# Nine more idle products of the identity in each early pause of TensorE

## The chip, the cores and the metric

The kernel runs on one core of one Trainium2 chip. The metric is the device time of one execution in microseconds (us). The time before the change is 676.36 us, the median of 3 runs that lie between 675.13 and 676.87 us.

## What is computed

Local attention with a summary of every block, then a two-layer feed-forward network, in float32:

```python
# q, k, v: (4, 8, 768, 64); w_in: (512, 2048); w_out: (2048, 512)
k_sum = k.reshape(B, H, nb, block, D).max(axis=3)
v_sum = v.reshape(B, H, nb, block, D).mean(axis=3)
scores_l = scale * np.matmul(q, k.transpose(0, 1, 3, 2))     # kept where |i - j| < 16
scores_s = scale * np.einsum('bhsd,bhnd->bhsn', q, k_sum) + np.log(block)
a = softmax(concatenate([scores_l_masked, scores_s]))
x = matmul(a, concatenate([v, v_sum]))                       # reshaped to (3072, 512)
h = x @ w_in
g = h * (1.0 / (1.0 + np.exp(-h)))
return g @ w_out
```

## The kernel before

**Tiles.** The 3072 tokens are cut into 24 stages of 128 tokens for the attention and into 12 chunks of 256 tokens for the network. A stage computes scores of a pair of heads (line 602, later 593 or 595 and 596), the softmax (VectorE line 609, ScalarE line 612, the scaling at 623, 625 or 627), turns the weights round (lines 636 and 638 on TensorE, or a transposing DMA at line 654) and multiplies with v (lines 668 or 683). Two stages fill one chunk x, which is kept as a high and a low part (xh at lines 696 and 701, xl at lines 697 and 702). The network walks over 16 slices f of the hidden layer: twelve matmuls of the first layer into a bank h (line 757), tanh and product on ScalarE and VectorE (767, 768, 769), six matmuls of the second layer (762). The weights come in 64-bit form and are decoded on ScalarE and VectorE (716 to 723, 256 to 263).

**Order.** Nothing runs in the order of the source. Every piece is given to a planner as an operation with its engines, its cost and what it reads and writes. `sweep` walks through planned time and gives each engine its sequence; `issue` then writes the instructions in the order of planned start, and each engine runs its own sequence in that order. Semaphores hold an instruction until its data are there. DMAs are issued by SyncE (SP), also in one sequence.

**Idle products.** Where the plan leaves TensorE without work it puts in matmuls whose result nobody reads: the identity, read as 16-bit numbers, times itself, 128x256. They exist so that TensorE is not idle. In the early part, before the first operation of the network, each pause gets as many as fit, counted at 110 ns each, and they write bank 0 (line 333). Afterwards only pauses ahead of the network's first layer get them, and they write the bank h that this layer is about to write (line 766), so they wait until the last reader of that bank is done. In the program there are 131 of them in 11 places: 15, 17, 1, 19, 2, 8, 1 and 18 at line 333, then 19, 20 and 11 at line 766. Pause 1 is the place with the first 15, pause 10 the place with the 20. In the sequence of TensorE an idle product stands like any other instruction: whatever is behind it starts after it, even if its data have come.

The number of products is the last entry of a planned operation:

```python
for _ in range(fills):
    (self.ops[i][6] or self.fill)()
self.ops[i][1](e)
```

Of the kernel before, what the change touches and what calls it, by code (L numbers as in the profile page):

```python
# [87 lines left out]
class Plan:  # L88
# [10 lines left out]
    BUSY = 3072.0  # L99
    FILL = (110.0, 256.0)  # L100
    GUARD = 150.0
    FIRST = 3000.0
    ROUNDS = 6
    SPARE = 100
# [41 lines left out]
    def sweep(self, prio, on, back):  # L146

        n = len(self.ops)
        before, after = [o[2] for o in self.ops], self.users
        if back:  # L150
            before, after = after, before
        left = [len(d) for d in before]
        end, chosen = [0.0] * n, [None] * n
        free = {} if back else {"dma": 1680.0}
        shared = 0.0
        ready, seen, fills, filled, early, order = {}, {}, 0, self.FIRST, True, []

        def arrive(i):
            ready[i] = {e: max([end[d] + (self.lag(e, chosen[d], d) if back else self.lag(chosen[d], e, i)) for d in before[i]], default=0.0)
                        for e in ((on[i],) if on else self.ops[i][0])}  # L160

        for i in range(n):
            if not left[i]:
                arrive(i)
        while ready:
            best = None
            for i, ts in ready.items():
                for e, s in ts.items():
                    f = free.get(e, 0.0)
                    t = max(s, f, shared) if e in self.ops[i][5] else max(s, f)  # L170
                    wait = self.SPARE if e == "dve" and len(ts) > 1 and t < self.RUSH else 0.0
                    key = (max(t + wait, f + self.PATIENCE), prio[i], t + self.ops[i][0][e], i)
                    if best is None or key < best[0]:
                        best = (key, i, e, t)
            _, i, e, t = best
            del ready[i]
            cost, cols = self.ops[i][0][e], self.ops[i][4]
            fills = 0
            if e == "pe" and not back:
                early = early and cols < self.BUSY  # L180
                if early or self.ops[i][6]:
                    while True:
                        rate = 1.0 if seen.get(int(filled / self.TICK) - 1, 0.0) >= self.BUSY else 0.5
                        if filled + self.FILL[0] / rate + self.GUARD > t:
                            break
                        filled = self.stream(seen, filled, *self.FILL)
                        fills += 1
                stop = self.stream(seen, t, cost, cols)
                filled = stop
            else:  # L190
                stop = t + cost * (1.0 if e in ("pe", "dma") else self.MARGIN)
            end[i], chosen[i] = stop, e
            free[e] = stop
            if e in self.ops[i][5]:
                shared = stop
            order.append((t, stop, i, e, fills))
            for u in after[i]:
                left[u] -= 1
                if not left[u]:
                    arrive(u)  # L200
        return order
# [727 lines left out]
```

## Time and profile before

| | us |
|---|---|
| median of the runs (lowest, highest) | 676.36 (675.13, 676.87) |
| the profiled execution, as timed | 675.26 |
| its span, first to last instruction | 673.5 |
| TensorE (PE) busy | 657.9 |
| VectorE (DVE) busy | 490.1 |
| ScalarE (ACT) busy | 428.0 |
| GpSimd (POOL) busy | 198.3 |

The busy time of TensorE holds the idle products too. The mean granted clock of TensorE over the span is 0.989 of full speed; 1.00 is 2.4 GHz and 0.50 is 1.2 GHz. Times in the rows below are counted from the start of the span.

### The profile page before, as it was taken

The numbers are of one execution on the slowest core, as the hardware profiler recorded it, in microseconds if no ns is written. First come the engines' busy times: TensorE is split into PE (matmuls) and PEld (weight loads), VectorE is DVE, ScalarE is ACT, GpSimd is POOL, SyncE is SP. The second block draws the span as 40 slices with busy tenths as digits, with TensorE's granted clock in tenths as the row PEclk, the third lists the DMA queues.
The fourth block names the chain that finished last, engine by engine and source line by source line (L and its number), as shares of the span: only waits on it lengthen the run. The fifth ranks groups of instructions, "written<-read, shape, count | busy, mean of one in ns | idle before, by whom it ended". The sixth has DMA issues, their size and how long they took to land.

```text
span 673.5 us, 14263 instructions
## 1 busy us (share of the span) xinstructions
PE 657.9 (98%) x4995; PEld 572.4 (85%) x4995; DVE 490.1 (73%) x1538; ACT 428.0 (64%) x1122; POOL 198.3 (29%) x241
## 2 busy tenths in 40 slices
PE   7988999999999999999999999999999999999997
PEld 4666899887988898888988898888898888899996
DVE  6886978688899646887888755897899986433332
ACT  4977999788867754666755554765776853322322
POOL 3241255333343111332535141223335333000000
PEclk9987999999999999999999999999999999999999
DMA  8689793976654842573664752573744642100000
GB/s 299 223 237 277 272 313 109 238 202 179 165 155 130 230 132 83 150 173 78 182 155 121 194 170 78 125 188 92 178 125 139 158 88 40 44 1 1 32 0 33
DMA packets 101354, 97.42 MB, mean 145 GB/s; under 512 B 76950, under 2 KB 80022, under 8 KB 101282
## 3 DMA queue, kind: packets, MB, share of 16 engines
q1 hardware_dynamic: 101282, 96.51, 52.4%
q8 instruction: 39, 0.64, 0.4%
q14 instruction: 33, 0.27, 0.1%
HBM read 70.34 MB, written 6.29 MB: 114 GB/s over the span
## 4 chain that ended last, share of the span: by engine, by line
PE 92%; DVE 3%; ACT 2%; DMA 2%; issue 0%; SPq 0%; POOL 0%; ACTq 0%; POOLq 0%
PE bank L757 41%; PE bank L762 39%; PE bank L683 4%; PE bank L595 2%; PE bank L596 2%; DMA qk<-in_qkT_dram 1%; PE bank L593 1%; DMA raw<-in_kD_dram 1%; PE bank L526 1%; PE bank L766 1%; DVE e L609 1%; DVE p L651 1%; PE bank L602 1%; ACT e L612 0%; PE bank L333 0%
## 5 line engine op out<-in xcount | busy, mean ns | idle before, releaser
L757 PE MATMUL bank<-xh,wt 128*128 128x256 f32 x1536 | 309.8, 285 | 0.0
L757 PEld LDWEIGHTS bank<-xh,wt 128*128 128x128 f32 x1536 | 252.5, 191 | 8.2 <-issue 0.4
L762 PE MATMUL bank<-wt,gh 128*128 128x512 f32 x768 | 247.3, 403 | 0.0
L757 PE MATMUL bank<-xl,wt 128*128 128x256 f32 x768 | 217.8, 284 | 0.3 <-DVE xl L697 0.3
L263 POOL TENSOR_TENSOR gl<-t,gh 128x256 fp32r<-128x256 f32 x123 | 108.7, 884 | 320.3 <-ACT gh L769 245.9
L767 ACT ACTIVATE t<-bank 128x256 f32<-128x256 f32 x192 | 73.3, 382 | 125.2 <-PE bank L757 123.5
L757 PEld LDWEIGHTS bank<-xl,wt 128*128 128x128 f32 x768 | 147.1, 192 | 6.8 <-DVE xl L697 0.5
L768 DVE SCALAR_TENSOR_TENSOR t<-t,bank 128x256 f32<-128x256 f32 x192 | 80.0, 417 | 99.4 <-ACT t L767 98.0
L762 PE MATMUL bank<-wt,gl 128*128 128x512 f32 x384 | 150.2, 391 | 1.0 <-POOL gl L263 1.0
L762 PEld LDWEIGHTS bank<-wt,gh 128*128 128x128 f32 x768 | 129.8, 190 | 17.5 <-issue 0.6
L769 ACT CAST gh<-t 128x256 fp32r<-128x256 f32 x192 | 77.8, 406 | 64.5 <-DVE t L768 62.9
L651 DVE SCALAR_TENSOR_TENSOR p<-e,sum,p 128x128 f16<-128x128 f32 x352 | 115.4, 389 | 1.3 <-ACT p L623 0.8
L612 ACT ACTIVATE e<-e,mx 128x182 f32<-128x182 f32 x192 | 84.4, 442 | 12.6 <-DVE mx L609 12.2
L762 PEld LDWEIGHTS bank<-wt,gl 128*128 128x128 f32 x384 | 72.1, 188 | 18.1 <-POOL gl L263 1.7
L263 DVE TENSOR_TENSOR gl<-t,gh 128x256 fp32r<-128x256 f32 x69 | 30.7, 444 | 34.4 <-ACT gh L769 20.0
L609 DVE CUSTOM_DVE_ANT_0 e<-bank,masks,qsc 128x182 f32<-128x182 f32 x144 | 52.2, 400 | 2.8 <-PE bank L596 2.4
L625 POOL TENSOR_SCALAR p<-e,sum 128x182 f16<-128x182 f32 x46 | 23.2, 509 | 46.5 <-DVE sum L618 18.2
L612 ACT ACTIVATION_READ_ACCUMULATOR e<-e,mx 128x1 f32 x192 | 36.7, 191 | 0.0
L263 POOL TENSOR_TENSOR vv<-raw,vv 128x1024 f16<-128x1024 f32 x15 | 32.5, 2170 | 7.6 <-ACT vv L256 7.2
L683 PEld LDWEIGHTS <-vv 128*64 128x64 f16 x880 | 25.7, 111 | 5.6 <-issue 4.6
L595 PE MATMUL bank<-qk 128*128 128x182 f16 x144 | 28.7, 246 | 0.0
L498 DVE SCALAR_TENSOR_TENSOR qk<-raw,qsc,qk 64x1264 f16<-64x1264 f32 x18 | 28.0, 1555 | 0.7
(127 smaller groups left out, 696.8 us busy)
## 6 DMA issues: line engine op xcount, KB each, us to landing
wt<-in_w_dram SPq DMA_DIRECT2D x32, 512.0 KB
raw<-in_kD_dram SPq DMA_DIRECT2D x18, 632.0 KB
raw<-in_v_dram SPq DMA_DIRECT2D x20, 512.0 KB
raw<-in_qD_dram SPq DMA_DIRECT2D x18, 512.0 KB
out_dram<-raw SPq DMA_DIRECT2D x24, 256.0 KB
raw<-in_kF_dram SPq DMA_DIRECT2D x12, 384.0 KB
raw<-in_qF_dram SPq DMA_DIRECT2D x9, 512.0 KB
raw<-in_vR_dram SPq DMA_DIRECT2D x12, 384.0 KB
```

The costliest lines, as they stand in the source:

```text
L263: eng[e].tensor_tensor(out=out, in0=in0, in1=in1, op=ALU.subtract)
L498: plan.op({"dve": 1450}, lambda e: nc.vector.scalar_tensor_tensor(out=kst[64:, :, :NLOC], in0=kr[64:], scalar=qs[64:, 1:2], in1=kst[64:, : ...
L595: nc.tensor.matmul(out=sc[:, i, :NKEY], lhsT=qh[:, h, :], rhs=kst[:, h, :], start=True, stop=False)
L609: plan.op({"dve": 258 if b == 0 else 323}, lambda e, i=i: nc.vector.tensor_tensor_reduce(out=et[:, i, :], in0=sc[:, i, :NKEY], in1=mask, s ...
L612: plan.op({"act": 431}, lambda e, i=i, h=h: nc.scalar.activation(out=et[:, i, :], in_=et[:, i, :], func=AF.Exp, scale=-1.0, bias=mx[:, i:i ...
L651: nc.vector.scalar_tensor_tensor(out=pt[:, i, to:to + z - a], in0=et[:, i, a:z], scalar=su[:, i:i + 1], in1=pt[:, i, a:z], op0=ALU.mult, o ...
L683: nc.tensor.matmul(out=av[j * D:(j + 1) * D, i * P:(i + 1) * P], lhsT=vt[:, vi, h * D:(h + 1) * D], rhs=tt[:, j * 3 + blk, :], start=(n == ...
L757: nc.tensor.matmul(out=h, lhsT=wt[f, 0][:, part, ct * P:(ct + 1) * P], rhs=x[:, ct, :], start=(ct == 0 and q == 0), stop=(ct == NCT - 1 an ...
L762: nc.tensor.matmul(out=bank[ob[u]], lhsT=g[:, u * P:u * P + P], rhs=wt[f, 1][:, part, :], start=(opens and q == 0), stop=(closes and q == 2))
L767: plan.op({"act": 264}, lambda e: nc.scalar.activation(out=t, in_=h, func=AF.Tanh, scale=0.5), r=[("bank", k)], w=[("t", j)], prio=i - TUN ...
L768: plan.op({"dve": 335}, lambda e: nc.vector.scalar_tensor_tensor(out=t, in0=t, scalar=1.0, in1=h, op0=ALU.add, op1=ALU.mult), r=[("bank", ...
L769: plan.op({"act": 307}, lambda e: nc.scalar.copy(out=gh, in_=t), r=[("t", j)], w=[("gh", n)], prio=i - TUNE["post"])
```

## The change

Whenever a pause got at least one product and the operation behind it is planned to start before 75,000 ns, nine more products (1000 divided by 110, rounded down) are added to the count. They are added after the plan has worked out its times, so that the planned times do not know of them.

```diff
@@ class Plan
     GUARD = 150.0
+    OVER, BUSIER = 1000.0, 75000.0
     FIRST = 3000.0
@@ def sweep
                         filled = self.stream(seen, filled, *self.FILL)
                         fills += 1
+                    if fills and t < self.BUSIER:
+                        fills += int(self.OVER / self.FILL[0])
                 stop = self.stream(seen, t, cost, cols)
```

Pauses 1 to 10 get nine more each, pause 11 none: 131 products become 221. Apart from them the sequence of every engine is what it was, and the lines of the changed kernel are three higher (333 is 336, 602 is 605, 757 is 760).

TensorE at pause 3, in the middle of the early attention, between a small transpose for the scale of v and the turning round of softmax weights (`ident` is the identity, `e` the softmax weights, bank_199 is bank 0). Before:

```order
L431 MATMUL bank_205<-ident,am 1x128
L333 LDWEIGHTS ident
L333 MATMUL bank_199<-ident 128x256
L636 MATMUL bank_202<-ident,e_174 128x128 x2
L638 MATMUL bank_202<-ident,e_174 54x128 x2
```

The same place in the changed kernel:

```order
L434 MATMUL bank_205<-ident,am 1x128
L336 LDWEIGHTS ident
L336 MATMUL bank_199<-ident 128x256
...
L639 MATMUL bank_202<-ident,e_174 128x128 x2
L641 MATMUL bank_202<-ident,e_174 54x128 x2
```

The line of dots stands for nine more pairs of a weight load and a product: one product has become ten, and nothing else stands there.

TensorE at pause 10, between the scores of a stage (`qk` holds q and k) and the first layer for the third slice (`wt` the weights, `xh` the chunk). Before, with 19 more pairs in place of the dots:

```order
L602 MATMUL bank_203<-qk_150 128x182
L602 MATMUL bank_204<-qk_150 128x182
L766 LDWEIGHTS ident
L766 MATMUL bank_199<-ident 128x256
...
L757 MATMUL bank_199<-xh_184,wt 128x256
```

In the changed kernel, with 28 more pairs in place of the dots:

```order
L605 MATMUL bank_203<-qk_150 128x182
L605 MATMUL bank_204<-qk_150 128x182
L769 LDWEIGHTS ident
L769 MATMUL bank_199<-ident 128x256
...
L760 MATMUL bank_199<-xh_184,wt 128x256
```

Twenty products have become 29, all of them on the bank that the first layer behind them writes.

## Rows read from the trace of the kernel before

**Rows 1.** The page: busy time by engine, and engines' shares of the last chain
```profile
PE 657.9 (98%) x4995; PEld 572.4 (85%) x4995; DVE 490.1 (73%) x1538; ACT 428.0 (64%) x1122; POOL 198.3 (29%) x241
...
PE 92%; DVE 3%; ACT 2%; DMA 2%; issue 0%; SPq 0%; POOL 0%; ACTq 0%; POOLq 0%
```

**Rows 2.** Waits of TensorE from 64 us on: us, times, longest
```profile
PE bank L762 <- POOL gl L263: 1.0, 1, 1.0
```

**Rows 3.** Stretches: us, busy by engine (instructions), granted clock, DMA share, GB/s
```profile
24.00:28.00 4.00, 4.00 (x36) 3.30 (x34) 3.85 (x21) 3.83 (x13) 0.00 (x0) 1.00 0.49 163
...
44.00:48.00 4.00, 1.86 (x6) 1.49 (x6) 3.49 (x14) 3.44 (x8) 0.86 (x1) 0.59 0.94 292
48.00:52.00 4.00, 4.00 (x48) 3.78 (x49) 1.67 (x3) 1.42 (x3) 0.00 (x0) 0.55 1.09 289
...
56.00:60.00 4.00, 3.71 (x18) 2.58 (x18) 4.00 (x17) 4.00 (x13) 1.13 (x2) 0.50 1.29 298
```

**Rows 4.** TensorE in order of time, 0 to 20 us: start, duration, instruction, [idle before]
```profile
1.36 3.38 PE L333 MATMUL bank<-ident 128*128 128x256 bf16 x15 [1.36 <-POOL ident masks.py:199]
7.58 1.58 PE L602 MATMUL bank<-qk 64*128 64x182 f32 x8 [2.84 <-ACT qk L256]
9.10 2.75 PE L333 MATMUL bank<-ident 128*128 128x256 bf16 x17
11.78 1.04 PE L526 MATMUL bank<-wt,blocks 128*24 128x512 f32 x2
```

**Rows 5.** Half microseconds of pause 2, idle products alone
```profile
9.50:10.00 0.50, 0.50 (x4) 0.38 (x3) 1.00 1.07 390
...
11.00:11.50 0.50, 0.50 (x7) 0.44 (x6) 1.00 1.08 376
```

**Rows 6.** TensorE in order of time, 20 to 75 us
```profile
23.50 2.24 PE L333 MATMUL bank<-ident 128*128 128x256 bf16 x19
25.59 0.44 PE L636 MATMUL bank<-ident,e 128*128 128x128 f32 x2
...
27.15 1.04 PE L333 MATMUL bank<-ident 128*128 128x256 bf16 x8
28.34 0.89 PE L602 MATMUL bank<-qk 64*128 64x182 f32 x8
...
46.14 1.55 PE L593 MATMUL bank<-qk 64*128 64x182 f32 x4 [2.96 <-DMA qk<-in_qkT_dram]
...
56.29 4.42 PE L766 MATMUL bank<-ident 128*128 128x256 bf16 x20 [3.19 <-DVE t L768]
60.37 0.56 PE L757 MATMUL bank<-xh,wt 128*128 128x256 f32 x1
...
62.62 0.88 PE L593 MATMUL bank<-qk 64*128 64x182 f32 x4
```

**Rows 7.** ScalarE and then VectorE in order of time, early instructions
```profile
11.01 0.62 ACT L530 ACTIVATE raw<-wt 128x512 f32<-128x512 f32 x1
...
25.10 0.43 ACT L623 ACTIVATE e<-e,sum 128x182 f32<-128x182 f32 x1
...
27.86 0.42 DVE L260 COPY wt<-bank 128x256 f32<-128x256 f32 x1
...
31.76 0.35 DVE L609 CUSTOM_DVE_ANT_0 e<-bank,masks 128x182 f32<-128x182 f32 x1 [0.55 <-PE bank L602]
```

**Rows 8.** Chain that ended last, 0 to 70 us: start, duration, what
```profile
42.28 3.72 DMA qk<-in_qkT_dram
...
47.69 2.87 PE bank L757 x12
50.58 0.02 ACT t L767
...
55.91 0.34 DVE t L768
...
65.09 1.43 PE bank L757 x12
```

## The prediction

> **What bounds the kernel now.** I read the page first: TensorE is busy for 98% of the span and carries 92% of the chain that ended last [rows 1]. Then the waits of TensorE after the early part: from 64 us to the end there is a single one that is long enough to be listed, 1.0 us [rows 2]. So whatever time TensorE stands at when it gets to 64 us, it keeps to the end: nothing behind that point can give back a delay of several microseconds, and nothing is cheaper there. The question is only how late, or how early, TensorE leaves the first 64 us.
>
> In those 64 us TensorE has three real pauses: 2.84 us before the first scores [rows 4], 2.96 us at 46.14 (a DMA of q and k) and 3.19 us at 56.29 (VectorE's step on the first bank h) [rows 6]. The granted clock is low there too: 0.59 and 0.55 in the stretches from 44 to 52 us, and 0.50 from 56 to 60 us [rows 3]. Everywhere else between 9 and 43 us TensorE runs without a listed wait, because the idle products fill the pauses. What has to be found out is whether they fill them with room to spare or to the brim.
>
> **Price of a product.** Nineteen of them stand between 23.50 and the next instruction at 25.59 [rows 6]: 2.09/19 = 0.110 us at full clock. At the low clock fifteen take 3.38 us [rows 4]: 0.225 us. Nine more are therefore 0.99 us at full and 2.0 us at half clock.
>
> **Pause 1: nothing.** The 15 products end at 1.36 + 3.38 = 4.74, and the scores start at 7.58, after 2.84 us of waiting for ScalarE [rows 4]. Even 2.0 us more end before that. Without that cover they would cost 2.0.
>
> **Pause 2: +0.99.** The 17 products go from 9.10 to 11.78, where the matmul of line 526 follows without a wait [rows 4]. Its block of v is in place earlier: ScalarE's line 530 reads the same block from 11.01 on [rows 7]. So this pause is already overfilled, and nine more come on top. The lower bound is a clock gain. Products run at four in half a microsecond at 9.5 us and at seven at 11.0 us [rows 5], so the clock is granted in between (the clock column holds no record before that change and prints 1.00). If pause 1 being busier brings this forward to before 7.58, the scores take 0.89 [rows 6] in place of 1.58 us [rows 4], and 26 products take 2.86 in place of 2.68: 0.5 us earlier. I take +0.99, since the row shows the clock rising only within TensorE's first long unbroken run and pause 1 still ends in a wait.
>
> **Pauses 3 to 7: +4.64.** Behind pause 4, line 636 starts at 25.59; the softmax weights it needs come from ScalarE's line 623, which ends at 25.10 + 0.43 = 25.53. Behind pause 6, the scores start at 28.34; VectorE's line 260, which clears their bank, ends at 27.86 + 0.42 = 28.28 [rows 6, 7]. The pauses are filled to 0.06 us. Five times nine products are 4.95 us, less the little room in pause 6: its eight products end at 27.15 + 8 x 0.110 = 28.03, which leaves 0.31. Can the others take this up? VectorE and ScalarE are busy for 3.85 and 3.83 of 4.00 us at 24 to 28 us [rows 3], and VectorE's line 609 at 31.76 sits idle for 0.55 us until the scores ahead of it are done [rows 7]. So they fall behind with TensorE. The cost is between +1.0 (see the second rival) and +4.95.
>
> **Pauses 8 and 9: nothing.** They lie between 33 and 41 us and cost TensorE 1.98 us, but behind them stands the wait of 2.96 us at 46.14, which ends when a DMA issued at 42.28 lands [rows 6, 8]. That DMA stands in SyncE's sequence behind the transposes of VectorE's softmax weights, so it moves with VectorE (by the terms above), not with these two pauses. The wait shrinks from 2.96 to about 1.0 us. Without that cover: +1.98.
>
> **Pause 10: +0.99.** Its 20 products do not fill the wait of 3.19 us at all: they write the bank that VectorE's line 768 still reads, so the first one starts after it, at 56.29, and the first layer follows at 60.37 [rows 6]. Everything here is in TensorE's own way. These 20 run at half clock. If the clock rises at the same time as before, the nine more push network matmuls out of the slow stretch as far as they fall into it themselves, so the price is that at full clock, 0.99. The upper bound is 2.0.
>
> **Clock at 46 us: -2.11.** After the wait of 2.96 us the stretches from 44 to 52 us ran at 0.59 and 0.55 [rows 3]. With a wait of about 1.0 us I expect the clock to hold. Then line 593 takes 0.88 (as at 62.62) in place of 1.55, and twelve matmuls of line 757 take 1.43 (as at 65.09) in place of 2.87 [rows 6, 8]: 0.67 + 1.44 = 2.11 us. This is on the path: ScalarE's line 767 starts at 50.58, as these twelve end at 47.69 + 2.87 = 50.56, and the chain goes on through ScalarE and VectorE to line 768, which releases pause 10 [rows 8]. The bounds are 0 and -2.11.
>
> [...]
>
> **Sum.** 0.99 + 4.64 + 0.99 - 2.11 = +4.51 us. On the profiled execution's 675.26 us that is 679.8; that execution is 1.1 us below the median of the runs, on which it would be 680.9. I say **680.0 us**, slower.
>
> **Rivals.** *First, the clock gives nothing back.* Where the clock falls depends on where TensorE's busy and idle stretches lie, and a wait of 1.0 us may still cost it. Then the sum is +6.62: 681.9. For it: 0.59 came after a wait of the same kind. Against it: that one was three times as long.
>
> *Second, the pauses swallow it.* The recorded chain has pieces of DMA, ScalarE and VectorE ahead of the waits at 46.14 and 56.29 [rows 8]. If those engines have room and do not fall behind, the DMA lands at 46.0 as before. But TensorE's own work has then grown by 0.99 + 4.64 + 1.98 = 7.6 us against a wait of 2.96, so it still comes to line 593 about 4.6 us late; with the clock held (line 593 and the twelve, -2.11) it is 2.5 us late at the next wait, and that one, 3.19 us, takes it all. Pause 10's 0.99 remains: 676.3, no change that can be measured. The point from which it decides is whether VectorE's line 609 is late by less than the wait it feeds. For it: TensorE is not on the chain just before 46 us. Against it: line 609's idle 0.55 us and the starts within 0.06 us.
>
> *Third, not slower at all.* As the second, and the clock also holds through the shortened wait before pause 10. Then 29 products take 3.19 us in place of the 4.08 from 56.29 to 60.37, and the twelve behind them run at full clock from the first (between 60.37 and 62.62 they took up to 2.25, less 1.43 is 0.8): -0.9 - 0.8 = -1.7 us, 673.6. It needs all of it at once: VectorE not late and the clock held in both places.
>
> *That the change does nothing* is excluded: 90 products more stand in TensorE's sequence.
>
> **Chances and range.** My forecast, between +2.5 (the clock also granted earlier in pause 2, some room on VectorE) and +5.6 us (pause 10 at half clock), 0.58; first rival 0.20; second 0.14; third 0.08. The forecast's own range is 677.8 to 681.9 with the higher median taken in. Over 0.3%, which is 2.0 us and about what runs spread over 1.7 us can tell from no change, are slower: the first rival and nearly all of the forecast, 0.76; within: the second and bits of its neighbours, 0.17; faster: the part of the third that reaches beyond its 1.7, 0.07. For 8 in 10 I go from 676.5, which takes in most of the second rival, to 682.8, the first rival with most of the median's 1.1.
>
> **What would show it.** Pause 2 right: line 529 (526 before) starts about 12.8 us, or 11.3 if the clock came early. Pauses 3 to 7 right: VectorE's line 612 (609 before) waits longer for the scores, and VectorE's and ScalarE's busy shares between 24 and 36 us fall. Pauses 8 and 9 right: the wait before line 596 (593 before) shrinks to 1 us and the DMA ahead of it is issued about 5.5 us later. Clock right: over 0.9 in the 5 us behind that wait. Pause 10 right: its products still start only behind VectorE's line 771. The forecast is wrong if TensorE's second-layer matmuls reach their unbroken run at the same time as before, or if waits appear behind 64 us.

## The result

The changed kernel takes 678.98 us (median of 16 runs, 676.97 to 681.66), the kernel before 674.98 us on the same chip (16 runs, 672.43 to 676.87): ratio 1.0064, interval [1.0049, 1.0080], that is +4.3 us [3.3, 5.4]. It is slower, by about the 4.5 us of the sum.

Executions of one and the same kernel can lie 4 to 8 us apart here, and one trace is one of them. The recorded execution of the changed kernel is the fastest of its 16 (676.97 us, span 675.2); the one of before (675.26 us, span 673.5) is a usual one by its time. So the two traces differ by 1.7 us only. Below, the traces tell what each step does, the medians what it costs. Two executions of the run with ten products in pause 10, at 1622 and 3602 us, are left out of its ratio.

The page of the changed kernel, the rows that answer to [rows 1]:

```profile
PE 663.2 (98%) x5085; PEld 577.4 (86%) x5085; DVE 494.7 (73%) x1538; ACT 426.4 (63%) x1122; POOL 197.6 (29%) x241
...
PE 87%; DVE 5%; DMA 4%; ACT 1%; SPq 1%; issue 1%; POOL 0%; ACTq 0%; DVEq 0%
```

TensorE is 5.3 us busier (663.2 against 657.9), though 90 products at 0.110 us are 9.9 us: most of the rest is work that ran at the full clock instead of the half one, as the rows below show piece by piece. Its share of the chain falls from 92 to 87%. Ahead of the wait for q and k the chain passes through VectorE and the DMA in both kernels, past pauses 8 and 9; what is new is that it comes there from TensorE's scores behind pause 7 (ends at 35.80), where before it came through ScalarE's line 612 (from 30.04).

Waits of TensorE in the first 64 us of the changed kernel (us, times, longest):

```profile
PE bank L769 <- DVE t L771: 2.1, 1, 2.1
PE bank L605 <- ACT qk L259: 1.8, 1, 1.8
PE bank L596 <- DMA qk<-in_qkT_dram: 1.4, 1, 1.4
...
PE bank L686 <- DMA wt<-p: 0.9, 1, 0.9
```

All three long waits of before are shorter (2.8, 3.0 and 3.2 us there [rows 4, 6]), and one is new, before line 686. From 64 us on no wait is listed at all.

For the steps, four more rows of TensorE in the kernel before, in order of time (start, duration, instruction):

```profile
30.84 0.89 PE L602 MATMUL bank<-qk 64*128 64x182 f32 x8
...
42.90 0.28 PE L757 MATMUL bank<-xh,wt 128*128 128x256 f32 x1
...
50.48 1.81 PE L683 MATMUL bank<-wt,vv 128*64 128x128 f16 x40
...
63.43 0.73 PE L762 MATMUL bank<-wt,gh 128*128 128x512 f32 x2
```

and TensorE in the changed kernel, the same places:

```profile
1.36 4.30 PE L336 MATMUL bank<-ident 128*128 128x256 bf16 x24 [1.36 <-POOL ident masks.py:199]
7.42 0.89 PE L605 MATMUL bank<-qk 64*128 64x182 f32 x8 [1.76 <-ACT qk L259]
8.24 3.01 PE L336 MATMUL bank<-ident 128*128 128x256 bf16 x26
11.18 1.04 PE L529 MATMUL bank<-wt,blocks 128*24 128x512 f32 x2
...
34.86 0.89 PE L605 MATMUL bank<-qk 64*128 64x182 f32 x8
...
48.34 0.28 PE L760 MATMUL bank<-xh,wt 128*128 128x256 f32 x1
49.99 0.85 PE L596 MATMUL bank<-qk 64*128 64x182 f32 x4 [1.38 <-DMA qk<-in_qkT_dram]
...
52.38 1.03 PE L686 MATMUL bank<-wt,vv 128*64 128x128 f16 x30
54.36 0.47 PE L686 MATMUL bank<-wt,vv 128*64 128x128 f16 x10 [0.95 <-DMA wt<-p]
...
58.15 4.99 PE L769 MATMUL bank<-ident 128*128 128x256 bf16 x29 [2.15 <-DVE t L771]
62.90 0.36 PE L760 MATMUL bank<-xh,wt 128*128 128x256 f32 x1
...
64.50 0.88 PE L596 MATMUL bank<-qk 64*128 64x182 f32 x4
```

Start against start (after less before), this is a ledger of the delay between the two traces:

| place in TensorE's sequence | before | after | late by | step |
|---|---|---|---|---|
| line 526 / 529, behind pause 2 | 11.78 | 11.18 | -0.60 | -0.60 |
| scores behind pause 7 | 30.84 | 34.86 | +4.02 | +4.62 |
| last matmul before the wait for q and k | 42.90 | 48.34 | +5.44 | +1.42 (pauses 8, 9) |
| scores behind that wait | 46.14 | 49.99 | +3.85 | -1.59 (wait) |
| weights times v, line 683 / 686 | 50.48 | 52.38 | +1.90 | -1.95 (clock) |
| products of pause 10 | 56.29 | 58.15 | +1.86 | -0.04 |
| first layer behind them | 60.37 | 62.90 | +2.53 | +0.67 |
| next scores, line 593 / 596 | 62.62 | 64.50 | +1.88 | -0.65 |

From the last line to the end of the span both kernels need the same: 673.5 - 62.62 = 610.9 and 675.2 - 64.50 = 610.7 us. So the difference of the traces arises ahead of 64 us, and nothing behind gives more than 0.2 us of it back.

The ledger compares one execution with one. The traces of the experiments below say how far such a step is a draw. Line 526 / 529 / 530 (first row) starts between 11.54 and 12.87 us in the nine traces whose pauses 1 and 2 are those of before (middle one 12.46; the trace of before, 11.78, is an early one), and at 11.01, 11.15, 11.18 and 13.23 in the four that have nine more in both. From the scores behind the wait for q and k to the weights times v (fourth to fifth row) it is 4.34 us before and 2.39 in the changed kernel.

Stretches of the changed kernel, with the columns of [rows 3]:

```profile
24.00:28.00 4.00, 4.00 (x37) 3.47 (x35) 3.11 (x17) 2.24 (x9) 0.00 (x0) 1.00 0.75 214
...
48.00:52.00 4.00, 2.62 (x20) 2.24 (x19) 3.55 (x14) 3.36 (x8) 0.85 (x1) 1.00 1.07 359
52.00:56.00 4.00, 2.76 (x52) 2.15 (x52) 2.52 (x5) 3.27 (x7) 0.00 (x0) 1.00 1.17 286
56.00:60.00 4.00, 1.85 (x15) 1.51 (x14) 4.00 (x20) 4.00 (x14) 2.00 (x3) 0.89 1.12 287
60.00:64.00 4.00, 4.00 (x26) 3.23 (x25) 4.00 (x14) 3.72 (x8) 0.52 (x2) 0.69 1.12 326
```

VectorE and ScalarE fell from 3.85 and 3.83 busy us to 3.11 and 2.24 between 24 and 28 us: they wait for scores that now come later, behind the idle products. The granted clock is 1.00 from 48 to 56 us, where it was 0.55 from 48 to 52 before. The two stretches in which pause 10 lies show 0.89 and 0.69.

### The profile page after: what moved, and what is told of

It reads as the page before. It is cut to its first block, busy times and chain, and to the rows that moved or that the text cites. A ratio compares the mean times of both kernels' runs of the same rounds, so it can differ in the third digit from the quotient of the medians.

```text
span 675.2 us, 14443 instructions
## 1 busy us (share of the span) xinstructions
PE 663.2 (98%) x5085; PEld 577.4 (86%) x5085; DVE 494.7 (73%) x1538; ACT 426.4 (63%) x1122; POOL 197.6 (29%) x241
## 4 chain that ended last, share of the span: by engine, by line
PE 87%; DVE 5%; DMA 4%; ACT 1%; SPq 1%; issue 1%; POOL 0%; ACTq 0%; DVEq 0%
PE bank L760 37%; PE bank L765 36%; PE bank L686 3%; PE bank L598 2%; PE bank L336 2%; DVE p L654 2%; PE bank L599 2%; DMA raw<-in_qF_dram 1%; DMA qk<-in_qkT_dram 1%; PE bank L596 1%; PE bank L769 1%; DMA raw<-in_v_dram 1%; PE bank L529 1%; DMA raw<-in_qD_dram 1%; DVE e L612 1%
## 5 line engine op out<-in xcount | busy, mean ns | idle before, releaser
L266 POOL TENSOR_TENSOR gl<-t,gh 128x256 fp32r<-128x256 f32 x123 | 106.7, 867 | 321.7 <-ACT gh L772 247.3
L266 DVE TENSOR_TENSOR gl<-t,gh 128x256 fp32r<-128x256 f32 x69 | 32.8, 475 | 32.9 <-ACT gh L772 19.1
L266 POOL TENSOR_TENSOR vv<-raw,vv 128x1024 f16<-128x1024 f32 x15 | 33.9, 2262 | 7.7 <-ACT vv L259 7.3
```

The costliest lines, as they stand in the source:

```text
L266: eng[e].tensor_tensor(out=out, in0=in0, in1=in1, op=ALU.subtract)
```

## The experiments

Every kernel is the kernel before with a table of extra products by pause, added where the instructions are issued; the rest of every engine's sequence stays as it is. Its lines are four higher than before (602 is 606, 766 is 770). The common edit is

```diff
+    MORE = {...}
...
-        last, seen = {}, 0
+        last, seen, pause = {}, 0, 0
         for _, _, i, e, fills in sorted(self.schedule(), key=lambda o: o[0]):
+            if fills:
+                pause += 1
+                fills += self.MORE.get(pause, 0)
```

and each run below is told by its table. Differences in us are the ratio less one, times 674.

### The steps one by one

**Pauses 3 to 7.**
```diff
+    MORE = {3: 9, 4: 9, 5: 9, 6: 9, 7: 9}
```


> Nine more products in pauses 3 to 7 alone (45 in all). Theory, that VectorE and ScalarE fall behind with TensorE because the scores come later: 5 x 0.99 less 0.31 = +4.6 us, the wait ahead of line 593 stays near 3 us, and so the clock gives nothing back; between +4 and +5.3. Rival, that VectorE and ScalarE have room and the two waits at 46 and 56 us take up TensorE's delay: 4.6 against 2.96 + 3.19, so 0, and the wait ahead of line 593 is gone.

Measured: 678.44 us against 673.86, ratio 1.0078 [1.0051, 1.0106], +5.3 us [3.4, 7.1]. The step is there and of the size said; that the pauses swallow it is out, and with it the third rival, which needs the same.

**Twice as much in the same pauses.**
```diff
+    MORE = {3: 18, 4: 18, 5: 18, 6: 18, 7: 18}
```


> Eighteen more products in pauses 3 to 7 (90 in all). Theory: a straight line, 10 x 0.99 less 0.31 = +9.6 us, since the room is used up by the first of them. Rival, that part of the delay is taken up by other engines or by the clock: less than twice the run with nine.

Measured: 683.13 us against 673.32, ratio 1.0140 [1.0124, 1.0157], +9.4 us [8.4, 10.6]. A straight line within the intervals: 0.104 us for each of the 90 products. VectorE shows who waits, in the changed kernel first:

```profile
35.78 0.35 DVE L612 CUSTOM_DVE_ANT_0 e<-bank,masks 128x182 f32<-128x182 f32 x1 [1.56 <-PE bank L605]
```

and in this one:

```profile
42.77 0.35 DVE L613 CUSTOM_DVE_ANT_0 e<-bank,masks 128x182 f32<-128x182 f32 x1 [2.54 <-PE bank L606]
```

This row reads the scores behind pause 7; before, it waited for them 0.55 us (line 609 at 31.76 [rows 7]). The first nine products in that pause add 1.56 - 0.55 = 1.01 us to the wait (the run with nine in pauses 3 to 7 alone shows 1.56 too) and the next nine 2.54 - 1.56 = 0.98, which is nine times 0.11: nothing of them is swallowed.

**Pauses 8 and 9.**
```diff
+    MORE = {8: 9, 9: 9}
```


> Nine more products in pauses 8 and 9 alone (18 in all). Theory: their 1.98 us lie inside the wait of 2.96 us ahead of line 593, so they cost nothing, and if the clock holds through the 1 us that is left of it, 2.1 us come back: between -2.1 and 0. Rival, that every added product costs its 0.11 us wherever it stands: +2.0 us.

Measured: 674.64 against 673.86, ratio 1.0008 [0.9989, 1.0028], +0.5 us [-0.7, +1.9]. No cost can be measured, as said; the rival's +2.0 lies just outside. TensorE in its trace:

```profile
45.38 0.85 PE L597 MATMUL bank<-qk 64*128 64x182 f32 x4 [0.85 <-DMA qk<-in_qkT_dram]
...
53.58 3.70 PE L770 MATMUL bank<-ident 128*128 128x256 bf16 x20 [2.70 <-DVE t L772]
...
59.45 0.74 PE L766 MATMUL bank<-wt,gh 128*128 128x512 f32 x2
```

The wait is 0.85 us in place of 2.96, the scores behind it run at the full clock, and pause 10 is released at 53.58 in place of 56.29. But that execution is the fastest of its twelve (671.19 us), and the median shows no gain.

**Pauses 1 and 2.**
```diff
+    MORE = {1: 9, 2: 9}
```


> Nine more products in pauses 1 and 2 alone. Theory: pause 1 costs nothing and may bring the clock forward, pause 2 is overfilled and costs 0.99 us at the same clock: between -0.6 (as in the profiled execution of the changed kernel, where line 529 starts at 11.18 in place of 11.78) and +1.0. Rival, that the clock is not touched by pause 1: +1.0 in every execution. If the parts add up, this run and the other three of this group sum to the +4.0 us of the whole change, but for the clock gain that needs pauses 3 to 9 together.

Measured: 673.07 against 673.86, ratio 0.9992 [0.9968, 1.0016], -0.5 us [-2.2, +1.1]. The +0.99 of the forecast lies in the interval, at its edge; the clock's part is shown further down.

**All but pauses 8 and 9.**
```diff
+    MORE = {1: 9, 2: 9, 3: 9, 4: 9, 5: 9, 6: 9, 7: 9, 10: 9}
```


> The change without its part in pauses 8 and 9. Theory: the same delay as the whole change, but the wait ahead of line 593 is 3 us again, so the clock gain of up to 2.1 us is not had: between 0 and 2.1 us slower than the whole change, so +4 to +6.1 us against the kernel before. Rival, that every product costs: 2.0 us faster than the whole change, so +2.0.

Measured: 678.34 against 673.32, ratio 1.0084 [1.0061, 1.0107], +5.7 us [4.1, 7.2]. With them it is +4.3 [3.3, 5.4]: pauses 8 and 9 give back about 1.4 us in the company of the others, with intervals that overlap. It points the way that was expected, but neither its size nor its sign is shown by these two runs.

### Pause 10

**Nine more there alone, and the same again.**
```diff
+    MORE = {10: 9}
```


> Nine more products in pause 10 alone. Theory: the products start only when VectorE has released their bank, so they lie in TensorE's way in full: +1.0 us (9 x 0.11; up to +2.0 at half clock). Rival, that the wait of 3.19 us ahead of them covers them: 0.

Measured: 678.14 against 673.86, ratio 1.0060 [1.0036, 1.0085], +4.0 us [2.4, 5.7] where +1.0 was expected. A miss, so it was run again:

> Nine more products in pause 10 alone, a second time. First theory, the price is real and not that of the products but of where the slow clock lies behind them: +3 to +5 us again. Rival, the price is that of the products at full or half clock and the first measurement was a chance of few runs: +1 to +2 us. In either case the products start only behind the VectorE step that reads their bank, and in a run that is slow by 4 us the trace shows either a longer slow stretch between 56 and 75 us or waits behind 64 us.

Measured: 676.30 against 674.12, ratio 1.0043 [1.0018, 1.0067], +2.9 us [1.2, 4.5]. The price is real, and in both runs the whole interval lies above the 0.99 us of the products at full clock; their 2.0 at half clock lie within the second. Its trace does not show it, however:

```profile
45.62 1.55 PE L597 MATMUL bank<-qk 64*128 64x182 f32 x4 [2.32 <-DMA qk<-in_qkT_dram]
...
55.74 4.72 PE L770 MATMUL bank<-ident 128*128 128x256 bf16 x29 [2.81 <-DVE t L772]
60.22 0.37 PE L761 MATMUL bank<-xh,wt 128*128 128x256 f32 x1
...
62.62 0.74 PE L766 MATMUL bank<-wt,gh 128*128 128x512 f32 x2
```

The products start behind VectorE, as said, 29 of them take 60.22 - 55.74 = 4.48 us, and the first layer behind them runs at the full clock. The second layer comes at 62.62. Its twelve executions fall into two heaps, six from 673.9 to 675.3 us and six from 677.3 to 680.5; the first run has two of its eight below 675.4 and six above 677.4. The traced executions are both of the lower heap (674.79, and 674.36, the fastest of its eight). What the upper heap does has not been recorded.

**Eighteen more, ten fewer, none at all.**
```diff
+    MORE = {10: 18}
```


> Eighteen more products in pause 10 alone (38 in place of 20). If each costs its own time, it is 0.99 us (full clock) above what nine more cost: about +2 to +5, by what the repeated run of nine gives. If it is the place of the slow stretch that costs, eighteen need not cost more than nine: +4 or less. If the cost of nine goes on in a straight line: +8.

Measured: 677.64 against 674.12, ratio 1.0043 [1.0027, 1.0060], +2.9 us [1.8, 4.0]: no more than nine more cost.

```diff
+    MORE = {10: -10}
```


> Ten products in place of 20 in pause 10, nothing else. Taking all 20 away gave 0. If the products pay for themselves through the clock as far as the 20th, this is 0 as well (within 0.7 us). If each costs 0.11 us and something of a fixed size is lost once the pause has none at all, it is -1.1 us.

Measured: 674.33 against 674.12, ratio 0.9998 [0.9980, 1.0015], -0.1 us [-1.3, +1.0]: nothing that can be measured. TensorE:

```profile
57.52 2.29 PE L770 MATMUL bank<-ident 128*128 128x256 bf16 x10 [2.76 <-DVE t L772]
...
62.31 0.74 PE L766 MATMUL bank<-wt,gh 128*128 128x512 f32 x2
```

```diff
+    MORE = {10: -20}
```


> The kernel before without any product in pause 10 (20 fewer). Theory: they fill no wait, since they begin when it has ended, and only stand in the way of the network's first layer for 4.1 us at half clock; without them that work starts 4.1 us earlier, but runs at half clock for the about 4 us in which they used to be the ones that ran slowly: 4.1 - 2.0 = -2.0 us. Rival, that the products bring the full clock and so pay for themselves: 0, or slower if the clock stays low longer without them.

Measured: 673.63 against 673.32, ratio 1.0000 [0.9987, 1.0013], where -2.0 was expected. A miss, and its trace shows where part of a gain can go. TensorE in order of time:

```profile
55.71 0.55 PE L761 MATMUL bank<-xh,wt 128*128 128x256 f32 x1 [2.79 <-ACT e L616]
...
59.42 0.74 PE L766 MATMUL bank<-wt,gh 128*128 128x512 f32 x2
```

and its waits behind 64 us:

```profile
PE bank L687 <- DMA tt<-p: 0.8, 1, 0.8
PE bank L597 <- DVE mx L613: 0.6, 1, 0.6
PE bank L599 <- DVE mx L613: 0.2, 1, 0.2
PE bank L597 <- DMA qk<-in_qkT_dram: 0.2, 1, 0.2
```

The first layer starts 4.7 us before its place in [rows 6] (60.37) and the second 4.0 us before (63.43), but then TensorE finds the others not ready: waits of 1.8 us in sum behind 64 us, where there was one of 1.0 [rows 2]. The span (671.3) is shorter by 2.2 in this execution, the median not at all. It need not go so: in the trace of pauses 8 and 9 the second layer starts as early (59.45), and the rest of the span takes 669.5 - 59.45 = 610.1 us as before (673.5 - 63.43 = 610.1); here it takes 611.9.

So in the medians pause 10 costs the same at 0, 10 and 20 products and about 3 us more at 29 and 38: a step, not a slope. The trace of the run with 38 is of a median execution (677.64 us), so it may be read for the price. TensorE:

```profile
56.54 5.97 PE L770 MATMUL bank<-ident 128*128 128x256 bf16 x38 [2.45 <-DVE t L772]
...
64.67 0.74 PE L766 MATMUL bank<-wt,gh 128*128 128x512 f32 x2
...
185.41 0.47 PE L687 MATMUL bank<-tt,vv 128*64 128x128 f16 x10 [1.67 <-DMA tt<-p]
```

Here the second layer comes 2.05 us later than in the run with 29 (62.62), and a wait of 1.67 us for a transposing DMA stands at 185 us, which the trace of before does not have. With 29 that wait was 0.83 us in the trace above. Whether the upper heap has more of such waits is open.

Within the pause itself the traces show a slope and no step. From the start of the products to the second layer it is 62.31 - 57.52 = 4.79 us with 10 products; with 20, 59.45 - 53.58 = 5.87 in the run of pauses 8 and 9, 5.90 in that of 3 to 7 and 6.07 in that of 1 and 2; with 29, 6.88 and 7.15 in the two runs here, 7.16 in the changed kernel and 7.16 without pauses 8 and 9; with 38, 64.67 - 56.54 = 8.13. That is (8.13 - 4.79)/28 = 0.12 us for each product. These are single traces, and the clock does not fall and rise at the same place in all. Two kinds with 20 stand apart: before itself needs 63.43 - 56.29 = 7.14, with its 20 at the half clock (0.50 [rows 3]), and two runs (all but pause 10, and twice as much in pauses 3 to 7) need 4.5, with their 20 at the full one (last section). So these traces do not show the step of the medians in the pause; where the time goes is open.

**All but pause 10.**
```diff
+    MORE = {1: 9, 2: 9, 3: 9, 4: 9, 5: 9, 6: 9, 7: 9, 8: 9, 9: 9}
```


> Nine more in pauses 1 to 9, none in pause 10. If pause 10 costs what its products take, this is 1 to 2 us less than the whole change: about +2.5 us against the kernel before. If pause 10 costs its 4 us in the company of the others too, it comes out at 0. If it costs nothing there, since the clock is held by the eight pauses ahead, it is +4.0 as the whole change.

Measured: 679.31 against 674.12, ratio 1.0077 [1.0052, 1.0101], +5.2 us [3.5, 6.8]. That is not below the whole change (+4.3): in the company of the others pause 10 costs nothing that can be measured. Of the three answers, the second falls, that it costs its 4 us there; the first, 1 to 2 us, is made unlikely by the two intervals but not excluded.

**A faster one?** The parts that give back, without the parts that cost.
```diff
+    MORE = {1: 9, 8: 9, 9: 9, 10: -20}
```


> Nine more products in pauses 1, 8 and 9, none at all in pause 10. Theory: only the pauses that have room get more, and the one whose products stand in the way gets none: -2.0 for pause 10, 0 to -2.1 for the clock behind line 593, 0 to -1 for the clock ahead of pause 2: -2 to -5 us. Rival, that early products cost wherever they stand: 27 x 0.11 = +3.0 less 2.0 = +1.0.

Measured: 673.44 against 673.32, ratio 0.9990 [0.9965, 1.0016]. A miss: no gain. Its trace, which is that of its slowest execution (677.32 us), has three waits of 0.9 to 1.0 us behind 64 us, for VectorE, GpSimd and a transposing DMA. Five of its twelve executions (669.08 to 671.29) are faster than any of the 23 of the kernel before (672.12 and up), and what they do differently has not been recorded. In the median no version beat the kernel before.

## Why the prediction was right, and where not

| step | said | the two traces | the medians |
|---|---|---|---|
| pause 2 (with 1) | +0.99 | -0.60 (a draw, see the ledger) | -0.5 [-2.2, +1.1] |
| pauses 3 to 7 | +4.64 | +4.62 | +5.3 [3.4, 7.1]; doubled +9.4 [8.4, 10.6] |
| pauses 8 and 9 | 0 | inside the wait | +0.5 [-0.7, +1.9] |
| pause 10 | +0.99 | 0.67 - 0.65 = 0 | +2.9 and +4.0 alone, about -0.9 with the others |
| clock at 46 us | -2.11 | -1.95 | about -1.4 (not shown apart from noise) |
| sum | +4.51 | +1.88 | +4.3 [3.3, 5.4] |

**The main term held.** Starts within 0.06 us of the data they need, read for pauses 4 and 6, were taken to say that pauses 3 to 7 were full to the brim, and the busy shares of VectorE and ScalarE said that these could not make up for it. Both were read rightly, and the doubling shows the term by itself.

**Pauses 8 and 9 held** in mechanism. The DMA ahead of the wait was to be 5.5 us later; it was issued 4.0 later (chain of waits of the changed kernel; before it stood at 42.28 [rows 8]), since pause 2 was 1.6 us kinder than said between these two traces:

```profile
46.25 3.61 DMA qk<-in_qkT_dram
...
50.84 1.63 PE bank L760 x12
...
57.77 0.34 DVE t L771
```

**The clock term held in this trace**: the four scores take 0.85 us and the twelve 1.63, against 1.55 and 2.87 before. The reason given, that a wait of 1 us keeps the clock and one of 3 us loses it, holds as a tendency and not as a rule. In the four traces with nine more in pauses 8 and 9 the wait is 0.85 to 2.07 us, the scores behind it run at the full clock, and from them to the weights times v it is 2.39, 2.40, 2.41 and 3.60 us. In the ten traces without, the wait is 2.27 to 3.49 us and that stretch 3.64 to 4.34, but for one of 2.40. In both groups there is an exception (last section).

**Pause 2 was mis-sized.** The lower bound of -0.5 us, scores and 26 products at full clock, is what the trace has (-0.60). The choice of +0.99 rested on the clock rising only within TensorE's first long run. With 24 products in pause 1 it was up before the first scores in four traces of five; with 15 it was so in one of nine. In the trace of the run without pause 10 the same order gave 13.23 in place of 11.18, so +0.99 lies between two outcomes and was neither.

**Pause 10 is not settled.** Between the two traces 29 products and what follows take as long as 20 did and what followed (+0.67, then -0.65), but before is the slowest of six traces with 20. Against the three with 5.87 to 6.07 us, nine more cost about 0.8 to 1.3 us within the pause, which is near the 0.99 of the prediction. The medians agree with neither: alone the nine cost some 3 us, in the company of the others nothing that can be measured. So the step that did not hold is to carry the price of the pause to the end unchanged, and why it does not carry is open.

**The premise on 64 us held nearly.** From the second layer to the end the traces need 609.5 to 611.9 us, and only that of the attempt at a faster one 614.2. Delay stays to the end, as said. Time won is not always kept: without pause 10's products TensorE is 4.0 us early at the second layer and meets new waits, while in the trace of pauses 8 and 9 it is as early and keeps it. One small wait was passed over when the prediction called the stretch from 9 to 43 us free of listed waits: 0.28 us at 41.61, for VectorE. It lies ahead of the wait of 2.96 us and changes no term.

**The sum came out better than its terms, and that is in part luck.** The medians of the four parts alone add up to about 5.3 + 0.5 + 4.0 - 0.5 = 9.3 us (8.2 with the second run of pause 10), the whole is 4.3. The three without pause 10 do add up: 5.3 + 0.5 - 0.5 = 5.3, and the run of all but pause 10 has +5.2. It is pause 10 that does not. The rival that the clock gives nothing back (+6.62) lies outside the interval of the whole, but that alone does not refute it: with pause 2 at -0.5 and pause 10 at 0, pauses 3 to 7 give about the whole's +4.3 without any gain of the clock. What speaks against it are the traces (2.39 us in place of 4.34). That the whole's trace shows +1.88 and its median +4.3 may come in part from its being the fastest execution; no slower one of it was recorded.

## What to carry to other kernels

In these runs an idle product in an in-order sequence was free only where TensorE had to wait further on anyway, before the other engines needed anything from it. The sign to look for is a row: a start within hundredths of a microsecond of the data it needs says that the pause is full, and each further product then cost its whole 0.11 us, on the engines behind as well. Price such fillers by the wait that comes next, not by the pause that they stand in, and test the parts together: here three of four added up and the fourth did not. Where executions of one kernel spread by more than the effect, take what a step does from several traces and what it costs from the median, and say which execution each trace was. A ledger of one trace against one took the slow draw of pause 10 for its price.

## What the hardware showed that was not expected

**The same order and the same wait, and another clock.** TensorE at the start of the run that has nine more in all pauses but 10, whose order up to there is that of the changed kernel:

```profile
7.80 0.89 PE L606 MATMUL bank<-qk 64*128 64x182 f32 x8 [1.73 <-ACT qk L260]
8.62 4.68 PE L337 MATMUL bank<-ident 128*128 128x256 bf16 x26
13.23 1.04 PE L530 MATMUL bank<-wt,blocks 128*24 128x512 f32 x2
...
52.26 0.85 PE L597 MATMUL bank<-qk 64*128 64x182 f32 x4 [1.59 <-DMA qk<-in_qkT_dram]
...
61.67 2.34 PE L770 MATMUL bank<-ident 128*128 128x256 bf16 x20 [2.96 <-DVE t L772]
```

and its stretches, TensorE alone (us, busy, granted clock, DMA share, GB/s):

```profile
9.00:10.00 1.00, 1.00 (x6) 0.50 1.08 392
...
11.00:12.00 1.00, 1.00 (x7) 0.50 1.08 370
```

Behind a wait of 1.73 us the scores still run at the full clock, 2.4 GHz, and then the clock is at 1.2 GHz (0.50) for much of the 26 products: 4.68 us. In the changed kernel, behind 1.76 us, the same 26 take 3.01. This one difference is 1.7 us. Later likewise: a wait of 2.33 us was followed by scores of 0.85 us in the run of pauses 3 to 7 (full clock), one of 2.32 us by scores of 1.55 us in the second run of pause 10 (half clock):

```profile
50.77 0.85 PE L597 MATMUL bank<-qk 64*128 64x182 f32 x4 [2.33 <-DMA qk<-in_qkT_dram]
```

So the length of the last wait alone does not decide the clock in these rows. The Trainium skill (TensorE: Matmul & The Clock Gate, section "What's actually happening") says that the watch which sets TensorE's clock runs free of the kernel's start, so that the moment of the change differs from run to run. These rows are in keeping with that, though they do not show that watch itself. Two executions of one order stand 2.05 us apart at 13 us (11.18 and 13.23, of which 0.38 are an earlier lag of the scores); that this makes a good part of the spread of the times is likely but not shown.

**Twenty products at full clock in pause 10.** In the same run the clock had fallen behind the scores at 52.26 (0.50 from 54 to 56 us) and come back (1.00 from 57 us on), and behind a wait of 2.96 us its 20 products take 63.77 - 61.67 = 2.10 us, against 4.08 before. That execution was no faster for it (679.76 us): two waits of 1.2 and 1.0 us, for VectorE and ScalarE, stand behind 64 us in it. The run with 18 more in pauses 3 to 7 shows the same behind a still longer wait:

```profile
66.72 2.34 PE L770 MATMUL bank<-ident 128*128 128x256 bf16 x20 [3.44 <-DVE t L772]
```

In the changed kernel the products start behind a wait of only 2.15 us, and the clock falls within the first microsecond (0.55 from 59 to 60 us, 0.50 from 60 to 62). So in pause 10, too, the longest wait is not the one that lost the clock.
